# Hashed attention with an FFN beside it: GpSimd's subtractions, the hash products and a normalising multiply put at other places of a step

## The chip, the core and the metric

The program runs on one NeuronCore of a Trainium2 chip. TensorE multiplies matrices, VectorE (DVE), ScalarE (ACT) and GpSimd (POOL) work on whole tiles, and SyncE (SP) issues most transfers. Each engine takes its instructions strictly in the order in which they stand. The metric is the device time of one launch in microseconds. A profile is one such execution, recorded.

## The reference

```python
q_bits = (einsum('bhsd,dk->bhsk', q, proj) > 0)        # 6 sign bits per row: its bucket; the same for k
mask   = q_bucket[:, :, :, None] == k_bucket[:, :, None, :]
scores = where(mask, q @ k.T / 8, -1e9)
attn   = exp(scores - scores.max(-1)); attn /= attn.sum(-1) + 1e-9
x      = (attn @ v) as [3072 tokens, 512]               # 4 batches, 8 heads, 768 rows, 64 wide
h      = x @ w_in                                       # 512 -> 2048
out    = (h * clip(h + 3, 0, 6) / 6) @ w_out            # 2048 -> 512
```

All of it is in float32.

## The kernel before, in words

**Products.** TensorE multiplies float32 numbers as a high and a low part. The high part is a rounding copy (`hi`, made by ACT), the low part is what the copy lost (`lo = x - hi`, a subtraction by DVE or POOL). A product is then three matmuls, or two where one side carries both parts side by side.

**Attention.** There are 32 heads of 768 rows; a *step* `k` handles 128 query rows of one head, so a head has six steps and the program 192. What a step does is spread over its neighbours: at step `k` the scores of step `k + 3` are multiplied (`lead`, L937), the row minima of `k + 2` are taken (`lowest`, L360), the exponential of `k + 1` is formed (`exponential`, L371) and its result is turned in blocks of 32 by DVE and written to DRAM (`flip`, L395; tiles `f` and `fd`). `move` (L403) brings the turned probabilities of step `k` back in four transfers, in place as tile `spare` or `px`. Two steps later `split_p` (L420) splits them into `ph` and `pl`, in two halves: half 0 by ACT and DVE, half 1 by ACT and POOL (L442, L443). `values` (L457) then multiplies them with `v` into `acc`; it runs in even steps only, for two steps at once: twelve matmuls, alternately with `ph` (L465) and `pl` (L466).

**A new head.** When `k + 3` reaches the first step of a head, `split_qk` (L273) prepares the head after it: ACT copies (L295), three transfers repeat the high parts in other places (L296 to L298), and POOL subtracts the low parts of `k` (tile `kk`, L301) and of `q` (tile `qq`, L303). Later steps of the head load the raw tile of the next one (`get_qk`), split `v` (`split_v`, L336, L337, on POOL), multiply the hash (`hash_qk`, L305, six matmuls into the PSUM tile `z`), turn its signs into mask columns (`bits`, L314, DVE) and scale the next raw tile (`scale_q`, L267, ACT). The scores tile `s` and the hash tile `z` share one pair of PSUM banks here, so whichever comes next on TensorE waits until DVE has read the one before (`lowest` reads `s`, `bits` reads `z`).

**The FFN beside it.** From step 107 on, `beside_ffn` (L1005) writes one step of attention and one 128-column block of the FFN into each other by hand. A generator `ffn` (L827) is advanced at four stages: at A it splits the gated values (`gb`: ACT L601, POOL L602), at B it multiplies `h` (`gemm1`, L573 to L575), at C it multiplies the block before (`gemm2`, L611 to L613) and applies the gate (ACT L593, DVE L594), and at D it does one item of preparing the next 256 tokens (`beside`): broadcasting reciprocals (POOL L521), two transposes into `rt` (TensorE L531) and a multiply by `rt` (DVE L534). TensorE's row of a step is therefore: values (even steps), `h`, hash (one step in six), `po`, scores, `rt` (while tokens are prepared).

The order on TensorE, DVE, ACT and POOL is the order of this code; nothing is moved by a scheduler. SP takes the transfers in its own order. The flag `paced` is true inside `beside_ffn`, and `lows` collects the low-part subtractions of a step, which `split_lows` issues after `lead`.

Of the kernel before, what the change touches and what calls it, by code (L numbers as in the profile page):

```python
# [10 lines left out]
F32 = mybir.dt.float32  # L11
# [7 lines left out]
P = 128  # L19
# [9 lines left out]
LA = 3  # L29
# [14 lines left out]
def lsh_attention_moe(  # L44
# [10 lines left out]
    nc = tc.nc  # L55
# [3 lines left out]
    KT = S // P  # L59
# [197 lines left out]
    def spans(i: int):  # L257


        n = 4 if i <= 2 else 1  # L260
        return [slice(x * S // n, (x + 1) * S // n) for x in range(n)]
# [8 lines left out]

    copied = None

    def split_qk(i: int, copy):  # L273
# [25 lines left out]
        copied = last  # L299
        for c in spans(i + 1):  # L300
            nc.gpsimd.tensor_sub(k2[:D, c], raw[D:, c], q1[D:, c].bitcast(F32))  # L301
        for c in spans(i + 1):
            nc.gpsimd.tensor_sub(q2[D:, c], raw[:D, c], q1[:D, c].bitcast(F32))  # L303

# [115 lines left out]
    def split_p(g: int, c: int, third: bool):  # L420
# [23 lines left out]
        nc.scalar.copy(hi, pt)  # L444
        lows.append(lambda: engine.tensor_sub(lo, pt, hi.bitcast(F32)))  # L445

# [80 lines left out]
    def normalise(name: str, x, rb, tag: str | None = None):  # L527

        rt = bank([P, TC], f"rt{name}", tag)
        for u in range(TC // P):  # L530
            nc.tensor.transpose(  # L531
                rt[:, u * P : (u + 1) * P], rb[:, u].rearrange("p h d -> p (h d)"), ident[:]
            )
        nc.vector.tensor_mul(x, x, rt[:])  # L534

# [26 lines left out]

    def split_x(x, src, engine):
        nc.scalar.copy(x[0], src)  # L564
        engine.tensor_sub(x[1], src, x[0].bitcast(F32))  # L565
# [371 lines left out]
    def lead(j: int):  # L937
# [8 lines left out]
        if t == 2:  # L946
            if i:
                split_v(i)

            if n + 1 < NJ and n != H + 1:  # L950
                get_qk(n + 1)
# [5 lines left out]
        if t == 3 and n < NJ and alone:  # L957
            bits(n)
        if t == 4 and n + 1 < NJ:
            scale_q(n + 1)  # L960
# [28 lines left out]
    with tc.manual_schedule(engines={ET.PE, ET.DVE, ET.Activation, ET.Pool}):  # L989
# [9 lines left out]
        def go(part: str):  # L999
            if stage == part:  # L1000
                next(fill, None)
# [3 lines left out]
        def beside_ffn(k: int):  # L1005
# [24 lines left out]
            if k + 2 < NS:  # L1030
                lowest(k + 2)
            paced = True
            while through and (through[0] < vnext // 2 - 1 or k % 2 or k < GT):
                output(through.pop(0))
            if k + LA < NS and (k + LA) % KT == 2 and (k + LA) // KT + 1 < NJ:
                hash_qk((k + LA) // KT + 1)
                bits((k + LA) // KT + 1)
# [4 lines left out]
            if GT <= k < NS:  # L1042
                move(k)
            go("D")
            if k % KT in (2, 4):
# [124 lines left out]
```

## Time and profile before

| | us |
|---|---|
| median of 3 runs | 1073.55 |
| lowest and highest | 1073.17, 1077.03 |
| the profiled execution | 1075.23 |
| its span in the trace | 1073.5 |
| TensorE busy, mean granted clock | 992.4, 0.958 |
| VectorE, ScalarE, GpSimd busy | 690.5, 634.8, 530.8 |

The profiled execution spent 1.7 us outside its span. The page lists an instruction group with its busy time and, behind the bar, the idle time of its engine just before it with the instruction that ended it. `gb<-g,gb` reads "writes gb, reads g and gb". The clock column gives the TensorE clock that was granted, 1.00 being full speed. Roughly, the span has four parts: attention alone to 150 us, the FFN of the first batch to about 275 us, attention alone to about 420 us, attention beside the FFN (steps 107 and on) to about 885 us, and the rest of the FFN.

### The profile page before, as it was taken

The page shows a single profiled execution, that of the slowest core. Times are in us where ns is not written, and L with a number is a line of the kernel's source. Part 1 is how long each engine was busy: PE and PEld are TensorE (multiplying, and loading weights), DVE is VectorE, ACT ScalarE, POOL GpSimd, SP SyncE. Part 2 cuts the span into 40 slices and gives each one's busy share as a digit, 9 for nine tenths or more (in the row PEclk, how much of TensorE's full clock was granted, in tenths as well). Part 3 has the DMA queues.
Part 4 walks back from the last instruction along what each step waited for, and adds up shares of the span by engine and source line. Part 5 has one row for each costly group of instructions (what it writes and reads, how often), then busy time and mean ns, then how long its engine had stood idle before and what let it go on. Part 6 is the DMA issues. An engine that isn't in the chain of part 4 may idle for free.

```text
span 1073.5 us, 19263 instructions
## 1 busy us (share of the span) xinstructions
PE 992.4 (92%) x6342; PEld 901.1 (84%) x6342; DVE 690.5 (64%) x1350; ACT 634.8 (59%) x1418; POOL 530.8 (49%) x608
## 2 busy tenths in 40 slices
PE   8999999999999997788988898878988999999998
PEld 7998888888899986677877777877977888898997
DVE  7999988987599997556555565565654661233322
ACT  6888865555688885455555565555655663334332
POOL 6777726566277764555555545555555552200000
PEclk9999999999999998689998899889998999999999
DMA  4566586000355545666586667667666751001000
GB/s 125 147 148 161 142 308 221 1 1 6 104 114 118 121 119 158 197 184 203 161 226 194 198 182 208 186 201 227 188 175 195 216 163 48 22 18 41 1 21 20
DMA packets 107898, 146.78 MB, mean 137 GB/s; under 512 B 12644, under 2 KB 77540, under 8 KB 107800
## 3 DMA queue, kind: packets, MB, share of 16 engines
q1 hardware_dynamic: 103320, 140.06, 43.0%
q0 software_dynamic: 4480, 5.51, 4.5%
q8 instruction: 50, 0.82, 0.3%
q14 instruction: 48, 0.39, 0.1%
HBM read 74.98 MB, written 51.12 MB: 117 GB/s over the span
## 4 chain that ended last, share of the span: by engine, by line
PE 39%; DMA 5%; POOL 4%; issue 3%; DVE 3%; ACT 2%; SPq 2%; DVEq 0%; POOLq 0%; ACTq 0%
PE h L574 5%; PE h L575 5%; PE h L573 5%; PE po L611 5%; PE po L613 5%; PE po L612 5%; PE acc L466 3%; DMA fd<-f 2%; PE acc L465 2%; POOL qq L303 2%; SPq L78 2%; PE s L356 1%; PE s L358 1%; DVE f L398 1%; POOL pl L445 1%
## 5 line engine op out<-in xcount | busy, mean ns | idle before, releaser
L594 DVE SCALAR_TENSOR_TENSOR g<-g,h 128x256 f32<-128x256 f32 x192 | 80.5, 419 | 205.7 <-ACT g L593 205.1
L365 DVE TENSOR_SCALAR_CACHE_REDUCE p<-s 128x768 f32<-128x768 f32 x192 | 183.4, 956 | 26.3 <-PE pt L387 12.4
L593 ACT ACTIVATE g<-h,three 128x256 f32<-128x256 f32 x192 | 91.2, 475 | 177.3 <-PE h L575 154.5
L377 ACT ACTIVATE p<-p,m 128x768 f32<-128x768 f32 x192 | 179.6, 935 | 27.0 <-DVE p L365 26.3
L466 PE MATMUL acc<-pl,vv 128*128 128x256 f32 x564 | 149.7, 296 | 40.9 <-POOL pl L445 36.7
L465 PE MATMUL acc<-ph,vv 128*128 128x256 f32 x564 | 154.6, 303 | 3.3 <-DVE pl L445 3.3
L573 PE MATMUL h<-xh,w 128*128 128x256 f32 x512 | 151.2, 295 | 0.7 <-ACT xh L564 0.7
L466 PEld LDWEIGHTS acc<-pl,vv 128*128 128x128 f32 x564 | 111.2, 197 | 46.3 <-POOL pl L445 39.3
L575 PE MATMUL h<-xh,w 128*128 128x256 f32 x512 | 149.6, 292 | 0.0
L574 PE MATMUL h<-xl,w 128*128 128x256 f32 x512 | 149.4, 292 | 0.0
L602 POOL TENSOR_TENSOR gb<-g,gb 128x256 fp32r<-128x256 f32 x89 | 67.0, 752 | 127.6 <-ACT gb L601 127.6
L398 DVE STREAM_TRANSPOSE f<-p 128x768 f32<-128x768 f32 x84 | 82.0, 976 | 54.2 <-DMA fd<-f 39.6
L465 PEld LDWEIGHTS acc<-ph,vv 128*128 128x128 f32 x564 | 110.1, 195 | 6.6 <-issue 2.1
L356 PE MATMUL s<-kk,qq 76*128 76x384 f32 x384 | 103.0, 349 | 11.4 <-DVE p L365 8.0
L444 ACT CAST ph<-pt 128x384 fp32r<-128x384 f32 x208 | 93.1, 474 | 25.2 <-PE pt L387 14.3
L445 DVE TENSOR_TENSOR pl<-pt,ph 128x384 fp32r<-128x384 f32 x208 | 106.0, 549 | 2.5 <-ACT ph L444 1.9
L573 PEld LDWEIGHTS h<-xh,w 128*128 128x128 f32 x512 | 102.9, 201 | 2.7 <-ACT xh L564 1.0
L574 PEld LDWEIGHTS h<-xl,w 128*128 128x128 f32 x512 | 102.9, 201 | 1.7 <-DVE xl L565 0.2
L575 PEld LDWEIGHTS h<-xh,w 128*128 128x128 f32 x512 | 102.8, 201 | 0.0
L358 PE MATMUL s<-kk,qq 128*128 128x384 f32 x384 | 101.1, 345 | 0.0
L611 PE MATMUL po<-w,gb 128*128 128x512 f32 x242 | 100.0, 413 | 0.9 <-ACT gb L601 0.8
L613 PE MATMUL po<-w,gb 128*128 128x512 f32 x242 | 98.7, 408 | 1.2 <-POOL gb L602 0.9
(164 smaller groups left out, 2408.3 us busy)
## 6 DMA issues: line engine op xcount, KB each, us to landing
fd<-f SPq DMA_DIRECT2D x84, 384.0 KB, 2.9
spare<-fd SPq DMA_DIRECT2D x168, 96.0 KB, 2.3
px<-fd SPq DMA_DIRECT2D x168, 96.0 KB, 2.7
raw<-in_qkT SPq DMA_DIRECT2D x32, 384.0 KB, 4.3
kk<-qq SPq DMA_DIRECT2D x62, 192.0 KB, 3.1
wr<-in_w_in SPq DMA_DIRECT2D x16, 512.0 KB, 4.7
wr<-in_w_out SPq DMA_DIRECT2D x16, 512.0 KB, 11.1
vr<-in_v SPq DMA_DIRECT2D x32, 192.0 KB, 2.5
```

Of the source, the lines that this page charges most:

```text
L356: nc.tensor.matmul(s[:, c, :HW], lhsT=q1[:KM, us], rhs=half(k1[:KM], c), start=True, stop=False)
L358: nc.tensor.matmul(s[:, c, :HW], lhsT=q2[:, us], rhs=half(k2, c), start=False, stop=True)
L365: nc.vector.tensor_scalar(out=pr_[:], in0=s[:, :, :HW], scalar1=CAP, scalar2=None, op0=ALU.min, op1=ALU.min, accum_out=m[:],)
L377: nc.scalar.activation(pr_[:], pr_[:], AF.Exp, bias=m[:], scale=-1.0, accum_out=sms[b][:, t, h : h + 1])
L445: lows.append(lambda: engine.tensor_sub(lo, pt, hi.bitcast(F32)))
L465: nc.tensor.matmul(acc[:], lhsT=vv[:, kt], rhs=hi[:, x], start=(kt == 0), stop=False)
L466: nc.tensor.matmul(acc[:], lhsT=vv[:, kt], rhs=lo[:, x], start=False, stop=(kt == KT - 1))
L573: nc.tensor.matmul(hp[:], lhsT=wi[:, 0, wc], rhs=xh, start=(cc == 0), stop=False)
L574: nc.tensor.matmul(hp[:], lhsT=wi[:, 0, wc], rhs=xl, start=False, stop=False)
L575: nc.tensor.matmul(hp[:], lhsT=wi[:, 1, wc], rhs=xh, start=False, stop=(cc == NCC - 1))
L611: nc.tensor.matmul(po[u], lhsT=gh[:, us], rhs=wo[:, 0], start=(fc == 0), stop=False)
L613: nc.tensor.matmul(po[u], lhsT=gl[:, us], rhs=wo[:, 0], start=False, stop=(fc == NFC - 1))
```

## The change

All of it concerns steps in which `paced` is true, and there it does five things.

1. Where POOL makes a low part of the probabilities (half 1), the subtraction is issued directly behind ACT's copy in `split_p`. The one of DVE still waits for `split_lows`.
2. The two subtractions of `split_qk` go into a list `subs`. One is taken from it near the end of each step, after `split_lows` and `move` and before stage D, so the second runs one step later than the first.
3. `hash_qk` and `bits` run when `(k + 3) % 6` is 3, one step later than before. That step is even.
4. The load of the raw tile goes from the head's step 2 to its step 3, the scaling of it from step 4 to step 5.
5. The multiply by `rt` goes into a list `muls`; it is issued in the next step, behind `lowest`, or ahead of a split that needs it.

Three places of the order show it. On POOL, around a head's subtractions in the middle of the stage, this stood there (`gb` is the FFN's low part, `kk` and `qq` the head's, `pl` the probabilities', `spare<-rc` the broadcast):

```order
L602 TENSOR_TENSOR gb_0_10_6549<-g_0_10_6532,gb_0_10_6549 128x256
L301 TENSOR_TENSOR kk_6586<-raw_6351,qq_6587 64x768
L303 TENSOR_TENSOR qq_6587<-raw_6351,qq_6587 64x768
L445 TENSOR_TENSOR pl_1_6504<-px,ph_1_6503 128x3x128
L521 COPY spare<-rc_1_6480 128x256
L602 TENSOR_TENSOR gb_0_11_6624<-g_0_11_6583,gb_0_11_6624 128x256
L445 TENSOR_TENSOR pl_1_6631<-spare,ph_1_6630 128x3x128
```

and now this stands there:

```order
L621 TENSOR_TENSOR gb_0_10_6549<-g_0_10_6532,gb_0_10_6549 128x256
L452 TENSOR_TENSOR pl_1_6503<-px,ph_1_6502 128x3x128
L304 TENSOR_TENSOR kk_6587<-raw_6415,qq_6588 64x768
L530 COPY spare<-rc_1_6479 128x256
L621 TENSOR_TENSOR gb_0_11_6622<-g_0_11_6584,gb_0_11_6622 128x256
L452 TENSOR_TENSOR pl_1_6629<-spare,ph_1_6628 128x3x128
L304 TENSOR_TENSOR qq_6588<-raw_6415,qq_6588 64x768
```

The `pl` subtraction stands ahead of the head's, and the second of the head's stands behind the `pl` of the next step.

On DVE, some steps later, while tokens are prepared (`f` is the turn, `p` the minima, `qq<-z` the bits, `g` the gate, `pl` half 0, `xr` the multiply by `rt`), before:

```order
L534 TENSOR_TENSOR xr_1_6466<-xr_1_6466,rt_1_1_6673 128x256
L398 STREAM_TRANSPOSE f_6698<-p_6651 128x768
L365 TENSOR_SCALAR p_6703,m_6702<-s_6662 128x768
L321 TENSOR_SCALAR qq_6587<-z_6707,thr,val 44x768
L594 SCALAR_TENSOR_TENSOR g_0_13_6722<-g_0_13_6722,h_0_13_6685 128x256
L445 TENSOR_TENSOR pl_0_6628<-px,ph_0_6627 128x3x128
L534 TENSOR_TENSOR xr_1_6466<-xr_1_6466,rt_1_2_6741 128x256
L398 STREAM_TRANSPOSE f_6782<-p_6703 128x768
```

and now:

```order
L404 STREAM_TRANSPOSE f_6698<-p_6650 128x768
L371 TENSOR_SCALAR p_6703,m_6702<-s_6662 128x768
L543 TENSOR_TENSOR xr_1_6467<-xr_1_6467,rt_1_1_6673 128x256
L613 SCALAR_TENSOR_TENSOR g_0_13_6714<-g_0_13_6714,h_0_13_6685 128x256
L454 TENSOR_TENSOR pl_0_6626<-px,ph_0_6625 128x3x128
L404 STREAM_TRANSPOSE f_6771<-p_6703 128x768
L371 TENSOR_SCALAR p_6776,m_6775<-s_6720 128x768
L543 TENSOR_TENSOR xr_1_6467<-xr_1_6467,rt_1_2_6730 128x256
L327 TENSOR_SCALAR qq_6588<-z_6779,thr,val 44x768
```

The bits moved to the step behind, and each multiply by `rt` from the end of its step to the place behind the next step's minima.

The diff, whole but for lines of context:

```diff
@@ split_qk
         copied = last
-        for c in spans(i + 1):
-            nc.gpsimd.tensor_sub(k2[:D, c], raw[D:, c], q1[D:, c].bitcast(F32))
-        for c in spans(i + 1):
-            nc.gpsimd.tensor_sub(q2[D:, c], raw[:D, c], q1[:D, c].bitcast(F32))
+        for to, r in ((k2[:D], slice(D, P)), (q2[D:], slice(0, D))):
+            def low(to=to, r=r):
+                for c in spans(i + 1):
+                    nc.gpsimd.tensor_sub(to[:, c], raw[r, c], q1[r, c].bitcast(F32))
+            if paced:
+                subs.append(low)
+            else:
+                low()
@@ split_p
         nc.scalar.copy(hi, pt)
-        lows.append(lambda: engine.tensor_sub(lo, pt, hi.bitcast(F32)))
+        if engine is nc.gpsimd:
+            engine.tensor_sub(lo, pt, hi.bitcast(F32))
+        else:
+            lows.append(lambda: engine.tensor_sub(lo, pt, hi.bitcast(F32)))
@@ normalise
-        nc.vector.tensor_mul(x, x, rt[:])
+        muls.append(lambda: nc.vector.tensor_mul(x, x, rt[:]))
+        if not paced:
+            multiply()
+
+    muls = []
+
+    def multiply():
+        for f in muls:
+            f()
+        muls.clear()
@@ split_x
     def split_x(x, src, engine):
+        multiply()
@@ lead
         if t == 2:
             if i:
                 split_v(i)
+        if t == (3 if paced else 2):
             if n + 1 < NJ and n != H + 1:
                 get_qk(n + 1)
...
-        if t == 4 and n + 1 < NJ:
+        if t == (5 if paced else 4) and n + 1 < NJ:
             scale_q(n + 1)
@@ beside_ffn
             paced = True
+            multiply()
             while through and (through[0] < vnext // 2 - 1 or k % 2 or k < GT):
                 output(through.pop(0))
-            if k + LA < NS and (k + LA) % KT == 2 and (k + LA) // KT + 1 < NJ:
+            if k + LA < NS and (k + LA) % KT == 3 and (k + LA) // KT + 1 < NJ:
                 hash_qk((k + LA) // KT + 1)
                 bits((k + LA) // KT + 1)
...
             split_lows()
             if GT <= k < NS:
                 move(k)
+            if subs:
+                subs.pop(0)()
             go("D")
```

More of the change, by code (lines that the diff above doesn't have):

```diff
@@ L271, in lsh_attention_moe @@
     copied = None
+    subs = []
     def split_qk(i: int, copy):
```

## The prediction, made before the change was timed

> **What bounds the kernel now.** I read the page's first two parts first.
>
> ```profile
> PE 992.4 (92%) x6342; PEld 901.1 (84%) x6342; DVE 690.5 (64%) x1350; ACT 634.8 (59%) x1418; POOL 530.8 (49%) x608
> PEclk9999999999999998689998899889998999999999
> ```
>
> TensorE is busy for 92% of the span, and its clock reads below 9 only in slices 16 to 31 of 40, which is attention beside the FFN, the stage of the change. So I looked at that stage alone: what TensorE waited for between 470 and 820 us, most first (us, times, longest).
>
> ```profile
> PE acc L466 <- POOL pl L445: 35.6, 11, 3.6
> PE z L310 <- DVE p L365: 5.3, 4, 2.1
> PE s L356 <- DVE p L365: 2.4, 5, 0.7
> PE acc L466 <- DVE pl L445: 1.2, 2, 0.9
> ```
>
> One wait outweighs the rest: 35.6 us in eleven pieces of at most 3.6, in which the product with the probabilities' low part waits for POOL. The page's row of that product (idle time behind the bar) has 36.7 us of it in all, so nearly none lies outside this window.
>
> ```profile
> L466 PE MATMUL acc<-pl,vv 128*128 128x256 f32 x564 | 149.7, 296 | 40.9 <-POOL pl L445 36.7
> ```
>
> The timelines of POOL and TensorE show one of the eleven (start, duration, and in brackets the idle time before).
>
> ```profile
> 504.25 1.84 POOL L301 TENSOR_TENSOR kk<-raw,qq 64x768 fp32r<-64x768 f32 x1 [2.28 <-PE po L613]
> 506.14 1.80 POOL L303 TENSOR_TENSOR qq<-raw,qq 64x768 fp32r<-64x768 f32 x1
> 508.03 0.99 POOL L445 TENSOR_TENSOR pl<-px,ph 128x384 fp32r<-128x384 f32 x1
> 501.26 0.28 PE L573 MATMUL h<-xh,w 128*128 128x256 f32 x1
> 502.66 0.39 PE L611 MATMUL po<-w,gb 128*128 128x512 f32 x1
> 504.04 0.52 PE L356 MATMUL s<-kk,qq 76*128 76x384 f32 x2
> 509.07 0.58 PE L466 MATMUL acc<-pl,vv 128*128 128x256 f32 x1 [3.10 <-POOL pl L445]
> 510.31 0.41 PE L573 MATMUL h<-xh,w 128*128 128x256 f32 x1
> 512.87 0.63 PE L611 MATMUL po<-w,gb 128*128 128x512 f32 x1
> 515.32 0.52 PE L356 MATMUL s<-kk,qq 76*128 76x384 f32 x2
> ```
>
> POOL subtracts `kk` and `qq` of the next head for 3.6 us, and only then makes `pl`, which ends at 509.02; TensorE starts again at 509.07, 3.10 us late. The rows behind the wait are slower too. The twelve `h` matmuls took 1.40 us from 501.26 to 502.66 and 2.56 from 510.31 to 512.87; the six `po` matmuls 1.38 and 2.45. That is half clock, which the windows of 6.5 us behind each of the eleven waits confirm (us; busy PE, PEld, DVE, ACT, POOL; granted clock; DMA share). The first, the third and the last are shown.
>
> ```profile
> 475.60:482.10 6.50, 6.50 (x27) 6.05 (x28) 1.87 (x3) 2.27 (x6) 2.41 (x3) 0.58 0.48 127
> 545.00:551.50 6.50, 6.46 (x34) 6.09 (x34) 1.91 (x4) 2.31 (x5) 3.18 (x5) 0.74 1.06 261
> 816.20:822.70 6.50, 6.48 (x25) 5.96 (x26) 1.85 (x3) 1.91 (x5) 2.44 (x3) 0.53 0.67 186
> ```
>
> Seven of the eleven read 0.53 to 0.59, four 0.74. TensorE is busy in all of each window, so the lost clock is lost time.
>
> Last, how fast the stage runs without this. From the first resumption after such a wait to the eleventh there are ten heads; behind them, no head being left to split, comes a stretch of eight steps, from one turn of DVE (L398) to the eighth after it.
>
> ```profile
> 475.60:816.20 340.60, 297.99 (x1772) 269.91 (x1772) 195.39 (x345) 192.08 (x434) 181.77 (x203) 0.92 0.68 196
> 834.80:869.10 34.30, 33.21 (x220) 30.55 (x219) 23.73 (x45) 22.52 (x54) 17.23 (x22) 1.00 0.65 199
> 834.76 0.98 DVE L398 STREAM_TRANSPOSE f<-p 128x768 f32<-128x768 f32 x1 [2.36 <-DMA fd<-f]
> 869.08 0.97 DVE L398 STREAM_TRANSPOSE f<-p 128x768 f32<-128x768 f32 x1
> ```
>
> The ten heads took 34.06 us each, 5.68 a step; the eight steps 4.29 each, TensorE busy for 33.21 of 34.30 us at clock 1.00. So the other engines and the transfers can keep TensorE full at 4.29 us a step when a head's preparation is absent. With one hash, six matmuls of 0.17 us (a row below), that is 6 x 4.29 + 1.03 = 26.8 us for a head, 7.3 less than now.
>
> **The change part by part.** *The `pl` subtraction ahead of the head's two (edits 1 and 2).* Nothing is added: the durations of POOL's groups in the stage stay.
>
> ```profile
> L445 POOL TENSOR_TENSOR pl<-px,ph 128x384 fp32r<-128x384 f32 x31 | 31.3, 1011 | 4.6 <-ACT ph L444 1.7 <-DMA fd<-f 1.5
> L301 POOL TENSOR_TENSOR kk<-raw,qq 64x768 fp32r<-64x768 f32 x11 | 21.0, 1911 | 22.5 <-PE po L613 13.9 <-issue 4.8 <-ACT qq L295 3.8
> L303 POOL TENSOR_TENSOR qq<-raw,qq 64x768 fp32r<-64x768 f32 x11 | 20.1, 1832 | 0.6
> L602 POOL TENSOR_TENSOR gb<-g,gb 128x256 fp32r<-128x256 f32 x61 | 45.8, 751 | 79.0 <-ACT gb L601 79.0
> ```
>
> In front of the `pl` that TensorE waits for, 1.91 + 1.83 = 3.74 us go away; the waits were 3.24 on average (35.6 / 11), so all of it goes: **-35.6**. Is `pl` then early enough? It needs ACT's copy of half 1. TensorE was done with the product before it at 505.97 at the latest (3.10 us ahead of 509.07), and POOL had stood idle for 2.28 us before 504.25: there is room for 1.01 us.
>
> The clock loss behind the waits goes with them. Seven windows lose about 0.44, four 0.26: (7 x 0.44 + 4 x 0.26) x 6.5 = 26.8 us of full-speed work. At half clock the rows above took 1.8 times, not twice, so a little less was lost in time: 26.8 x 0.44 / 0.5 = 23.6; I take **-24**. Bounds: none, if what remains of the waits still cools the clock, and 26.8.
>
> In sentences that the sum does without: the Trainium skill, page TensorE: Matmul & The Clock Gate, section HAM oscillation, has the array fall to half clock after idle gaps above about 3.4 us, its window running freely. By that a wait of 3.24, the average here, would cost no clock, and the term would be near nothing instead of 24, the time 1045. The rows disagree: half clock stands behind a wait of 3.10 us here, and behind all eleven. The trace's term stays.
>
> The two subtractions now stand elsewhere, 1.9 us each, at the ends of two steps. Behind the first stands `gb` (L602) of the next step, which TensorE asks for in the `po` group, behind twelve `h` and twelve value matmuls of the same shape, 2.8 us into the step. Behind the second stands the `gb` of a step without values, asked for 1.4 us into it. POOL waits 1.3 us a step for `gb`'s copy (79.0 / 61), so a subtraction delays `gb` by about 0.6, and the matmuls ahead hide that: nothing. If that cover is gone it is at most 1.9 us a head, 21 us. The hash needs `qq` only in the step after the next.
>
> *The hash in an even step (edit 3).* The hash waits until DVE has taken the minima from the shared banks.
>
> ```profile
> 518.91 0.40 PE L310 MATMUL z<-qq,pjl 128*108 128x384 f32 x1 [1.09 <-DVE p L365]
> 519.84 0.34 PE L312 MATMUL z<-qq,pjh 128*108 128x384 f32 x1
> DVE qq L321 <- PE z L312: 14.1, 10, 1.5
> ```
>
> In an odd step only the `h` matmuls (1.4 us) stand between the scores and the hash; in an even one 1.4 us of values come in addition. The four waits here were 1.1 to 2.1 us, so about 1.4 us of cover takes nearly all: **-5**. In exchange DVE waits longer for `z`, which already costs it 1.4 us a time (14.1 / 10), and its gate and low part come later in that step. Scores follow the hash by 1.4 us of `po`, the bits take 1.09 us: it fits. Bounds: -5.3 and, if DVE is late into the next, shorter step by all of the 1.4, +15.
>
> *The raw tile a step later (edit 4)*: loaded for two steps (9 us) ahead of its scaling.
>
> ```profile
> raw<-in_qkT SPq DMA_DIRECT2D x9, 384.0 KB, 4.3
> fd<-f SPq DMA_DIRECT2D x68, 384.0 KB, 3.0
> ```
>
> It lands 4.3 us after issue: nothing. *The multiply by `rt` (edit 5)* takes a wait off DVE.
>
> ```profile
> DVE xr L534 <- PE rt L531: 13.9, 16, 1.9
> DVE f L398 <- DMA fd<-f: 25.0, 19, 2.2
> ```
>
> 13.9 us in 16 pieces, off TensorE's path while TensorE is full: nothing, but DVE reaches its turn 0.9 us earlier in those steps. The PSUM bank of `rt` is held for about one step more. There are four banks in turn and two or three tiles a step, so it comes round after that.
>
> **What is late next.** The turn (`f`) may overwrite its tile only when the write before it has landed; DVE waited 25.0 us for that in 19 turns. The chain of a step is: turn 0.98, issue of the write, landing 3.0, that is 4.3 us with SP free; TensorE needs 26.8 / 6 = 4.47. They are nearly equal. A head's three copies and its raw load stand in SP's queue in just those steps whose stall vanishes, and there a write takes longer. I put the new waits at 1.0 us a head: **+11**. Bounds: 0, and 3.75 a head (rival A), +41; I stay nearer to the lower, because the eight full steps hold such writes too. Denser traffic is in it: a DMA share of 0.68 over 34.06 us becomes 0.68 x 34.06 / 29 = 0.80.
>
> **Sum**: 35.6 + 24 + 5 - 11 = 53.6. The profiled execution took 1075.23 us, 1073.5 in its span; 1075.2 - 53.6 = 1021.6. The median was 1.7 us below that execution, and the gain should show in the median as well, so I say **1021 us** (1073.55 - 53.6 = 1020; between the two). The first head of the stage, before 470 us, is left out; it lost about 1 us to the same wait. The FFN after 885 us has nothing of the change.
>
> **The rivals.**
>
> *A. The write of the turn paces half of the steps.* SP issues four transfers for `move` ahead of the next write.
>
> ```profile
> 577.99 1.74 SPq L78 DMA_DIRECT2D px<-fd  x4
> 441.30 0.45 SPq L78 DMA_DIRECT2D fd<-f  x1
> 446.32 0.98 DVE L398 STREAM_TRANSPOSE f<-p 128x768 f32<-128x768 f32 x1 [2.83 <-DMA fd<-f]
> 448.44 0.65 PE L310 MATMUL z<-qq,pjl 128*108 128x384 f32 x1 [3.57 <-DVE p L365]
> ```
>
> They take 1.74 us of SP. Where DVE's turn follows its low part at once, the chain is 0.98 + 1.74 + 3.0 = 5.72 us, 1.25 over TensorE's 4.47. In three steps of a head this makes 3.75 us, 41 over the stage: 1021 + 41 - 11 = **1051**. For it: 19 waits on that write already. Against it: the eight full steps above contain such writes as well. The Trainium skill, DMA: Bandwidth & Descriptors, section Queues, rings and completion order, says that each DMA engine takes one issuer's descriptors in ring order; by that the head's copies are served ahead of the write behind them. The rows agree: the write issued at 441.30 landed at 446.3, after 5.0 us instead of 3.0.
>
> *B. The stall returns at another place.* The last three rows are one: a late write, DVE idle for 2.83 us, TensorE for 3.57, and half clock behind it. That costs 3.57 + 24 / 11 = 5.8 us; one for each of eleven heads is 64 us, and the time stays at **1074**. It needs a landing some 2 us later than usual, which the three copies (192 KB each) and the raw load could bring; against it, none of the 19 waits between 470 and 820 us was longer than 2.2.
>
> *C. Slower.* The same mechanism twice a head, in the step of the copies and in that of the raw load: 22 x 5.8 = 127 instead of the 64 removed, **1137**. It decides where two writes of a head land over 5 us after their issue. At one a head it is B.
>
> *D. `pl` isn't the last thing that half 1 waits for.* If ACT's copy, behind its own waits, is late by 2 us, TensorE waits 2 instead of 3.24 and keeps its clock: 22 us stay, 1021 + 22 = **1043**. Against it: POOL's `pl<-px` waited for ACT 1.7 us in 31 times.
>
> **How the numbers follow.** My forecast 0.68 (own range 1007 to 1034: -11 for no new waits, -3 for the clock's upper bound; +13 for new waits of 2.2 a head), A 0.14 and D 0.08 (1034 to 1058), B 0.05, C 0.03, and 0.02 for a gain under 15 us from mixtures. The range 1005 to 1050 leaves out half of A, B, C and the mixtures above, 0.17, and about 0.03 below. A median can be told from no change at 0.5%, 5.4 us, so faster means below 1068: 0.68 + 0.22 + 0.02 = 0.92. Same 0.05, slower 0.03.
>
> **What would show it.** TensorE's wait on POOL's `pl` in the stage falls from eleven pieces to none or some below 1 us; the clock column reads 9 throughout the stage but for its first two slices; POOL shows `pl` directly behind ACT's copy and `gb` between the head's two subtractions; the hash waits for the minima for under 2 us in all; the stage runs at 4.7 to 4.9 us a step; the FFN behind it has its old length. I am wrong if TensorE's waits for `p` (L365 of before) grow past 25 us, which is A or B; if the clock stays below 0.9 though the waits went; or if `po` waits for `gb` in the step of a subtraction, which breaks the cover that I named.

## The result

The changed kernel took **1047.47 us** (median of four, 1045.37 to 1049.28) beside 1073.36 for the kernel before on the same chip, a ratio of 0.975, interval 0.972 to 0.979. It is faster, inside the range, and 26 us above the time of the likeliest case. About half of the forecast gain came. 1047 is next to the time of rival A, 1051.

The first two parts of the page of the changed kernel, in the rows that answer to those of before, and its chain by line:

```profile
PE 979.4 (94%) x6342; PEld 885.6 (85%) x6342; DVE 706.9 (68%) x1350; ACT 634.6 (61%) x1418; POOL 534.1 (51%) x608
PEclk9999999999999999699999999999998999999999
...
DMA fd<-f 6%; PE h L593 6%; PE h L594 5%; PE h L592 5%; PE pt L393 5%; PE acc L474 5%; PE acc L475 5%; PE po L630 5%; PE po L632 5%; PE po L631 5%; PE s L362 4%; PE s L364 4%; DMA px<-fd 3%; DVE p L371 3%; SPq L78 3%
```

The clock reads 9 in the stage but for slices 17 and 31, where before it was below 9 in eight. The chain that ended last names the write of the turn, `fd<-f`, first. To put both kernels on one footing I took ten heads of each, from hash to hash (length, busy PE, PEld, DVE, ACT, POOL, granted clock, DMA share, GB/s). Before:

```profile
448.40:790.00 341.60, 299.35 (x1768) 271.63 (x1768) 193.54 (x341) 189.99 (x428) 177.78 (x197) 0.91 0.67 195
```

After:

```profile
449.40:768.20 318.80, 286.33 (x1770) 255.86 (x1770) 207.12 (x342) 190.30 (x429) 183.20 (x200) 0.97 0.72 209
```

What TensorE waited for in the ten heads, before:

```profile
PE acc L466 <- POOL pl L445: 32.0, 10, 3.6
PE z L310 <- DVE p L365: 7.8, 4, 3.6
PE s L356 <- DVE p L365: 2.4, 5, 0.7
PE acc L466 <- DVE pl L445: 1.2, 2, 0.9
```

And after, all rows of the view:

```profile
PE z L316 <- DVE p L371: 14.1, 8, 4.4
PE s L362 <- DVE p L371: 11.0, 9, 3.6
PE acc L475 <- DVE pl L454: 2.4, 3, 1.4
PE po L632 <- POOL gb L621: 1.7, 4, 0.4
PE po L630 <- ACT gb L620: 1.5, 3, 1.0
```

POOL's `pl` is gone without a rest. In its place the hash (`z`) and the scores (`s`) wait 14.1 + 11.0 = 25.1 us for the minima (`p`, L371, once L365), which were 7.8 + 2.4 = 10.2.

A head takes 31.88 us instead of 34.16. Of the 22.8 us in ten heads, TensorE's busy time gave 13.0 (299.35 to 286.33, for the same work) and its idle time 9.8 (42.25 to 32.47). The idle time should have fallen by the 32.0 of the stall, and the waits for the minima took back 25.1 - 10.2 = 14.9 of it; the sum at the end of this document has the rest.

The clock rose from 0.91 to 0.97 and not to 1. Two of the new waits, by the timeline:

```profile
542.54 0.84 PE L362 MATMUL s<-kk,qq 76*128 76x384 f32 x2 [3.62 <-DVE p L371]
706.29 0.42 PE L316 MATMUL z<-qq,pjl 128*108 128x384 f32 x1 [4.42 <-DVE p L371]
```

And the 6.5 us behind each, and behind one of 1.62 us at 572.56 (its row stands below), of which the third number from the end is the clock:

```profile
542.60:549.10 6.50, 6.50 (x36) 6.45 (x37) 2.82 (x6) 3.41 (x7) 2.06 (x3) 0.74 0.59 191
572.60:579.10 6.50, 6.50 (x34) 6.18 (x35) 3.13 (x7) 3.30 (x7) 2.51 (x4) 0.74 0.74 256
706.30:712.80 6.50, 6.50 (x30) 5.88 (x31) 3.83 (x6) 2.54 (x7) 1.66 (x2) 0.74 0.32 99
```

Behind most of the shorter ones the clock is full. So the new waits are more than the old, but smaller, and only some of them still cool the array. Who is late is read from DVE's own waits in the ten heads:

```profile
DVE f L404 <- DMA fd<-f: 55.7, 31, 5.3
```

The same stretch of before had:

```profile
DVE f L398 <- DMA fd<-f: 26.4, 20, 2.3
```

The turn now waits 55.7 us for the write before it, twice the 26.4 of before, and once for 5.3. That is not all. The same views put a further 11.6 us of the turn's waits (2.1 before) down to ACT's `ph` and `gb`. In each of them the trace has the last part of the write landing 0.09 us ahead of the turn, as in the rows that name the write, so they are waits for the write too: 67.3 us against 28.5. Where the trace tells when a transfer landed (10 of the 71 writes from 480 to 860 us, and 5 of 68 before), the median is not longer (3.0 us before, as quoted in the prediction):

```profile
fd<-f SPq DMA_DIRECT2D x71, 384.0 KB, 2.7
```

What is longer is the way to the issue and the worst landings, as one head shows. The timeline of the changed kernel there, by engine (start, duration, idle time before in brackets):

```profile
564.74 0.98 DVE L404 STREAM_TRANSPOSE f<-p 128x768 f32<-128x768 f32 x1 [2.02 <-DMA fd<-f]
567.06 1.49 DVE L454 TENSOR_TENSOR pl<-spare,ph 128x384 fp32r<-128x384 f32 x1
570.43 0.98 DVE L404 STREAM_TRANSPOSE f<-p 128x768 f32<-128x768 f32 x1 [1.88 <-ACT ph L450]
575.84 0.98 DVE L404 STREAM_TRANSPOSE f<-p 128x768 f32<-128x768 f32 x1 [2.02 <-DMA fd<-f]
...
565.20 1.02 POOL L452 TENSOR_TENSOR pl<-spare,ph 128x384 fp32r<-128x384 f32 x1
566.29 1.84 POOL L304 TENSOR_TENSOR qq<-raw,qq 64x768 fp32r<-64x768 f32 x1
...
564.48 2.04 SPq L78 DMA_DIRECT2D px<-fd  x4
566.62 0.67 SPq L78 DMA_DIRECT2D fd<-f  x1
568.61 1.75 SPq L78 DMA_DIRECT2D spare<-fd  x4
570.46 0.38 SPq L78 DMA_DIRECT2D raw<-in_qkT  x1
571.44 0.34 SPq L78 DMA_DIRECT2D fd<-f  x1
...
572.56 0.62 PE L362 MATMUL s<-kk,qq 76*128 76x384 f32 x2 [1.62 <-DVE p L371]
```

Two things can be read here. First, the turn at 564.74 ends at 565.72, but SP is still issuing the four `move`s of `px`, and the write goes out at 566.62. Second, DVE's own `pl` (half 0) starts at 567.06 while POOL is in the head's second subtraction (`qq`, 566.29 to 568.13), and takes 1.49 us; the mean before was 0.55. It ends at 568.55, and SP's next `move` overwrites the tile that it reads, so it goes out at 568.61. Behind that stand the raw load (570.46) and the next write (571.44); the turn that needs this write's landing comes at 575.84, 4.40 us later. This write was issued 0.03 us behind the end of its turn (570.43 + 0.98), so what stands ahead of it can have made it land late, but not leave late. (The wait of 1.88 us that the row at 570.43 puts down to ACT is one of those for the write, issued at 566.62.) In all ten subtractions from `spare` that were held for over 1 us in the stage, the `move` came 0.06 to 0.07 us behind the end of the subtraction.

The collision is a consequence of the change that the prediction did not have. Before, both head subtractions ended ahead of POOL's `pl`, and DVE's `pl` of that kind took 551 ns on average over the 30 of the ten heads. So after the result there were two readings of the missing 26 us. One, called W below: rival A, the chain of turn, issue, landing and next turn paces the steps of the copies whatever else is done. Two, called P: the collision does it, and without it the forecast would have come. A third, called H, was the hash: in its even step it might be what pulled the minima apart.

### The profile page after: what moved, and what is told of

The parts are those of the page before. It is cut to its first block, busy times and chain, and to the rows that moved or that the text cites. A ratio compares the mean times of both kernels' runs of the same rounds, so it can differ in the third digit from the quotient of the medians.

```text
span 1045.8 us, 19273 instructions
## 1 busy us (share of the span) xinstructions
PE 979.4 (94%) x6342; PEld 885.6 (85%) x6342; DVE 706.9 (68%) x1350; ACT 634.6 (61%) x1418; POOL 534.1 (51%) x608
## 4 chain that ended last, share of the span: by engine, by line
PE 58%; DVE 13%; DMA 12%; ACT 6%; issue 5%; SPq 3%; POOL 3%; DVEq 0%; ACTq 0%; POOLq 0%
DMA fd<-f 6%; PE h L593 6%; PE h L594 5%; PE h L592 5%; PE pt L393 5%; PE acc L474 5%; PE acc L475 5%; PE po L630 5%; PE po L632 5%; PE po L631 5%; PE s L362 4%; PE s L364 4%; DMA px<-fd 3%; DVE p L371 3%; SPq L78 3%
## 5 line engine op out<-in xcount | busy, mean ns | idle before, releaser
L371 DVE TENSOR_SCALAR_CACHE_REDUCE p<-s 128x768 f32<-128x768 f32 x192 | 183.4, 955 | 26.9 <-PE pt L393 12.4
L475 PE MATMUL acc<-pl,vv 128*128 128x256 f32 x564 | 147.2, 292 | 6.3 <-DVE pl L454 6.1
L592 PE MATMUL h<-xh,w 128*128 128x256 f32 x512 | 146.8, 287 | 0.7 <-ACT xh L583 0.7
L593 PE MATMUL h<-xl,w 128*128 128x256 f32 x512 | 145.3, 284 | 0.9 <-POOL xl L584 0.7
L594 PE MATMUL h<-xh,w 128*128 128x256 f32 x512 | 144.9, 283 | 0.0
L593 PEld LDWEIGHTS h<-xl,w 128*128 128x128 f32 x512 | 98.3, 192 | 3.4 <-POOL xl L584 1.2
L592 PEld LDWEIGHTS h<-xh,w 128*128 128x128 f32 x512 | 98.5, 192 | 2.7 <-ACT xh L583 1.0
L632 PE MATMUL po<-w,gb 128*128 128x512 f32 x242 | 97.4, 403 | 3.0 <-POOL gb L621 2.4
L630 PE MATMUL po<-w,gb 128*128 128x512 f32 x242 | 96.6, 399 | 2.5 <-ACT gb L620 2.5
L594 PEld LDWEIGHTS h<-xh,w 128*128 128x128 f32 x512 | 98.1, 192 | 0.0
```

The costliest lines, as they stand in the source:

```text
L371: nc.vector.tensor_scalar(out=pr_[:], in0=s[:, :, :HW], scalar1=CAP, scalar2=None, op0=ALU.min, op1=ALU.min, accum_out=m[:],)
L475: nc.tensor.matmul(acc[:], lhsT=vv[:, kt], rhs=lo[:, x], start=False, stop=(kt == KT - 1))
L592: nc.tensor.matmul(hp[:], lhsT=wi[:, 0, wc], rhs=xh, start=(cc == 0), stop=False)
L593: nc.tensor.matmul(hp[:], lhsT=wi[:, 0, wc], rhs=xl, start=False, stop=False)
L594: nc.tensor.matmul(hp[:], lhsT=wi[:, 1, wc], rhs=xh, start=False, stop=(cc == NCC - 1))
L630: nc.tensor.matmul(po[u], lhsT=gh[:, us], rhs=wo[:, 0], start=(fc == 0), stop=False)
```

## The experiments

Unless a text says otherwise a ratio is against the kernel before, timed in the same group of runs, with its 95% interval; since its median moved between groups (1073.36, 1071.19, 1074.83), kernels of different groups are compared by ratio. A ratio of 0.01 is 10.7 us. The changed kernel stands at 0.975 [0.972, 0.979]. The expectations are on record as they were written, under the names that they give to the three readings above.

**Edit 1 alone**, in the kernel before:

```diff
-        lows.append(lambda: engine.tensor_sub(lo, pt, hi.bitcast(F32)))
+        if engine is nc.gpsimd:
+            engine.tensor_sub(lo, pt, hi.bitcast(F32))
+        else:
+            lows.append(lambda: engine.tensor_sub(lo, pt, hi.bitcast(F32)))
```

> The kernel before with edit 1 alone: POOL's low part of half 1 directly behind ACT's copy; the head's two subtractions, the hash, the raw tile and the multiply stay where they were. Theory W (once POOL's low part is early, the stage is paced by the write of the turn, which must land before the next turn): nearly the whole gain comes from this edit, 1046 to 1051 us, and DVE waits some 50 us or more for the write. Theory P (in the changed kernel the head's second subtraction holds up DVE's own subtraction, 1.8 us instead of 0.55, and so the transfers behind it): there is no such collision here, so it is faster than the changed kernel, 1038 to 1043. Theory H (the hash in the even step costs waits of its own): faster than the changed kernel too, TensorE's waits of the hash for the minima 5 to 8 us instead of 15.

1042.61 us, 0.973 [0.970, 0.977]. What TensorE waited for longest in its ten heads (445.3 to 757.5 us):

```profile
PE z L310 <- DVE p L365: 20.0, 11, 4.8
```

And DVE for the write:

```profile
DVE f L398 <- DMA fd<-f: 23.8, 19, 2.4
```

This one edit brings the whole gain; the four others together add nothing that can be told from zero. Here the subtractions don't collide (`pl<-spare` 552 ns). The turn's row for the write is no longer than before (23.8), but with the 14.1 us put down to ACT's `ph` and `gb`, which are waits for the write here too, it is 37.9 us against 28.5. So the waits for the write grow without the collision too, though less than in the changed kernel (67.3). The time is the one that P gave, yet it can't be told from the changed kernel's. H had 5 to 8 us of waits of the hash for its odd step; there are 20.0.

**The hash back in the odd step**, in the changed kernel:

```diff
-            if k + LA < NS and (k + LA) % KT == 3 and (k + LA) // KT + 1 < NJ:
+            if k + LA < NS and (k + LA) % KT == 2 and (k + LA) // KT + 1 < NJ:
```

> The changed kernel with edit 3 alone undone: hash and bits in the odd step again, the rest as changed. H: the waits of the hash for the minima fall from 15.3 us to 5 or 6 and the time by 6 to 10, to 1037 to 1041 us. W: the late minima then hold up the scores instead, the sum of the waits for the minima stays at 27 to 32 us and the time at 1045 to 1050. My prediction had this edit at -5, so by it 1052.

1047.42 us, 0.978 [0.974, 0.982]: no difference. TensorE's waits for the minima only change places, in its ten heads:

```profile
PE z L316 <- DVE p L371: 23.6, 9, 4.4
PE s L362 <- DVE p L371: 1.8, 4, 1.0
```

25.4 us instead of 25.1, nearly all now at the hash. So the hash's place is not what costs, and in this kernel it is not worth the 5 us forecast either.

**The head's subtractions in four pieces each:**

```diff
-                for c in spans(i + 1):
+                for c in spans(0 if paced else i + 1):
```

> The changed kernel, but each of the head's two subtractions in four pieces of 192 columns, so that DVE is held up by a piece and not by a whole subtraction. P: DVE's subtraction in that step takes 0.6 to 1.0 us instead of 1.5 to 1.8 and the time falls by 6 to 12 us, to 1036 to 1041. W: DVE's subtraction gets shorter, but the time stays within 3 us of 1047.

1039.08 us, 0.970 [0.965, 0.976]. In its ten heads DVE's `pl<-spare` took 626 ns on average, 916 in the changed kernel, so the hold is shorter. But the pieces of a head take POOL 5.07 us instead of 3.80, and a new wait for `gb` stands at `po`:

```profile
PE po L632 <- POOL gb L621: 10.7, 10, 1.5
```

The time is in P's range, but the interval overlaps with the changed kernel's, so alone this settles nothing.

**Both subtractions in one step**, at its end, so that the second meets no `pl` of DVE from `spare`:

```diff
-            if subs:
+            while subs:
                 subs.pop(0)()
```

> The changed kernel, but both of the head's subtractions at the end of the same step, the split in two steps undone. P: POOL then begins them behind DVE's subtraction of that step, the collision is gone and the time falls by 5 to 10 us, to 1038 to 1042. W: 1045 to 1050. If the split in two steps was needed, TensorE waits for POOL's gb or pl in the step behind, by up to 1.9 us a head, and the time is 1050 to 1065.

1032.48 us, 0.963 [0.960, 0.966]: 13 us faster than the changed kernel, with intervals apart, and more than P gave.

Its ten heads, and in the next view DVE's subtraction from `spare`:

```profile
449.30:754.70 305.40, 282.93 (x1773) 251.39 (x1771) 200.86 (x342) 190.04 (x428) 183.62 (x201) 0.99 0.75 218
```

```profile
L454 DVE TENSOR_TENSOR pl<-spare,ph 128x384 fp32r<-128x384 f32 x30 | 16.5, 551 | 0.1
```

The hold at `spare` is gone (part of it is now at `px`, 773 ns for 651), the clock is 0.99, and DVE still waits 35.9 us for the write, 55.9 with the rows that name ACT's `ph` and `gb`. Moving the second subtraction is worth about 13 us of the 26 missing, not all.

One more thing moves with it. The raw load overwrites the tile that the head's subtractions read, so it can't go before the second of them has ended. In the changed kernel SP issues it behind the four `move`s, 0.5 to 2.4 us ahead of the next write in each of the ten heads, and from the issue of that write to the turn that needs it there are 4.36 us on average. In this run the load goes ahead of the `move`s, 3.6 to 5.9 us before the write, and there are 3.43 us. SP in the same head as above:

```profile
561.80 0.38 SPq L78 DMA_DIRECT2D fd<-f  x1
562.27 0.38 SPq L78 DMA_DIRECT2D raw<-in_qkT  x1
564.21 1.75 SPq L78 DMA_DIRECT2D spare<-fd  x4
566.43 0.34 SPq L78 DMA_DIRECT2D fd<-f  x1
```

In the two further runs on the collision (the fill, and the second subtraction ahead of `pl`) the load goes early too, with 3.49 and 3.62 us. So these runs show what the place of the second subtraction costs. How much of it is the hold on DVE and how much the place of the raw load, none of them shows; in the run with four pieces, where the hold is short, the load still stood right ahead of the write in seven of ten heads.

**A fill with zeros instead of the second subtraction**, in its place of the changed kernel. The low part of `q` is left out of the scores and the hash:

```diff
             def low(to=to, r=r):
+                if paced and r.start == 0:
+                    nc.gpsimd.memset(to.bitcast(F32), 0.0)
+                    return
```

> The changed kernel, but in the stage beside the FFN the second of a head's subtractions (the low part of q) is replaced at its place by a fill with zeros, which reads nothing. It leaves the low part of q out of the scores and the hash of those heads. P (POOL's second subtraction holds DVE's own up): DVE's subtraction into pl takes 0.55 to 0.65 us on average instead of 0.93, the waits for the minima fall from 29.7 to below 18 us, and the time to 1028 to 1038 us, at or below the version with both subtractions in one step (1032.5). W (the write of the turn paces the stage whatever POOL does): DVE's subtraction gets shorter, the waits for the minima stay at 25 us or more, 1043 to 1048.

1036.06 us, 0.967 [0.963, 0.971].

The groups of POOL and, in the next view, of DVE:

```profile
L304 POOL MEMSET qq<- 64x768 f32 x10 | 7.4, 736 | 0.6
```

```profile
L457 DVE TENSOR_TENSOR pl<-spare,ph 128x384 fp32r<-128x384 f32 x30 | 16.5, 551 | 0.0
```

An instruction of POOL that reads nothing does not hold DVE: 551 ns. The two overlapped by only 0.03 to 0.45 us a head, though, where the second subtraction overlapped by 0.39 to 1.79. The run gains about 9 us, inside P's range, and the waits for the minima from 455 to 800 us are 18.0 us for 29.7. That is no more than moving the subtraction gave, though the whole 1.84 us of POOL's reading is gone too.

**One step, and the hash in the odd step** (both edits above):

> Both subtractions in one step (1032.5 us) and the hash back in the odd step. With the collision away the hash edit should show what it is worth. My prediction: the four to eleven waits of the hash come back at 1 to 2 us each, 1037 to 1045 us. If the waits for the minima only move between hash and scores, as they did in the changed kernel (1047.4 against 1047.5), 1031 to 1035.

1043.9 us, 0.975 [0.972, 0.979], as expected. With this run four kernels differ only in two edits:

| ratio to before | hash in the even step | hash in the odd step |
|---|---|---|
| subtractions in two steps | 0.975 (the change) | 0.978 |
| subtractions in one step | 0.963 | 0.975 |

TensorE's longest wait by its sum in the ten heads of the new kernel:

```profile
PE z L316 <- DVE p L371: 16.8, 11, 3.7
```

From the upper right corner neither edit alone gains more than 0.3%, and the two together 1.5%. With the hash odd TensorE waits 16.8 us at the hash anyway; with the subtractions in two steps it waits for late minima wherever the hash is. The hash's even place is worth 13 us once the second subtraction is moved, and nothing that shows before; and moving it is worth 13 us only with the hash in the even step.

**One step, and the multiply by `rt` where it was before** (edit 5 undone):

```diff
         muls.append(lambda: nc.vector.tensor_mul(x, x, rt[:]))
-        if not paced:
-            multiply()
+        multiply()
```

> Both subtractions in one step (1032.5 us) and the multiply by rt back at the end of its step. My prediction: DVE waits some 12 to 14 us for the transposes again, off TensorE's path, so 1031 to 1035 us. If the turn's start now decides (W), 16 multiplies that end 0.4 to 0.9 us later put the writes and the minima late, 1037 to 1046.

1035.89 us, 0.967 [0.964, 0.971] beside 0.963 [0.960, 0.966]: the intervals overlap, so edit 5 is worth 0 to some 5 us; the time lies between the two ranges. DVE's wait for `rt` is back with 9.6 us.

**The turn in place.** The tiles `f` and `p` have two buffers between them and are made alternately, so every turn writes the buffer that the write just before it reads. If DVE turns `p` where it lies, no tile `f` is needed, each `p` has a buffer to itself for two steps, and what has to wait for that write is the minima, which come one turn later (1.1 us). With both subtractions in one step:

```diff
-        x = sp.tile([P, S], F32, name=f"f{g}", tag="p", bufs=2)
-        nc.vector.transpose(x[:], probs.pop(g)[0][:].rearrange("p c k -> p (c k)"))
+        x = probs.pop(g)[0][:].rearrange("p c k -> p (c k)")
+        nc.vector.transpose(x, x)
         d = dp.tile([P, S], F32, name=f"fd{g}", tag="fd", bufs=4)
-        dma(out=d[:], in_=x[:])
+        dma(out=d[:], in_=x)
```

> Both subtractions in one step (1032.5 us), and the turn writes in place of what it reads, so that not the turn but the minima behind it, 1.0 us later, must wait for the write before. W: of DVE's 40 us of waits for the write in 29 pieces about 1 us each goes, TensorE's waits for the minima (9.5 us) halve, 1022 to 1029 us. If the transfers themselves are the bound (how much they move, not when), DVE's wait goes from the turn to the minima in full and the time stays at 1030 to 1035.

1021.44 us, 0.954 [0.951, 0.958], below the kernel without it by 9 us with intervals apart, and just below the range that W gave. The raw load goes ahead of the `move`s in both of these kernels, so this pair has the slack of the write alone.

**The second subtraction ahead of POOL's `pl`** of its step, everything else as in the change, so that it runs ahead of DVE's subtraction:

```diff
             go("A")
+            if subs:
+                subs.pop(0)()
...
-            if subs:
+            if len(subs) == 2:
                 subs.pop(0)()
```

> The changed kernel with one instruction of POOL at another place: the head's second subtraction stands in the same step as now, but ahead of POOL's low part of half 1 and not behind it, so it runs some 1.0 us and more before DVE's subtraction comes up. P: DVE's subtraction into pl takes 0.55 to 0.65 us on average in the tile where it now takes 0.93, and the time falls to 1028 to 1036 us. W: 1044 to 1049. If POOL's low part, now 1.9 us later in that step, is what the transfers behind it wait for, also 1044 or more.

1038.83 us, 0.967 [0.964, 0.970]: 9 us faster by the place of one instruction on POOL, but less than P expected. A part of the hold stays:

```profile
L454 DVE TENSOR_TENSOR pl<-spare,ph 128x384 fp32r<-128x384 f32 x30 | 19.1, 636 | 0.1
```

**The change with the turn in place**, the collision untouched:

> The changed kernel with the turn in place (the wait for the write goes from the turn to the minima behind it, 1.0 us later); the collision of POOL's second subtraction stays. If collision and write act one behind the other in the same step (the held subtraction makes the transfers late, the late transfers the turn), the gain is at least that of the one-step version (11 us): 1030 to 1037. If the collision alone decides, 1043 to 1048.

**1019.46 us**, 0.948 [0.945, 0.952].

Its ten heads, then DVE's subtraction, then DVE's wait for the write (now at the minima), then TensorE's waits for the minima:

```profile
446.50:739.20 292.70, 277.43 (x1771) 250.47 (x1772) 201.29 (x342) 188.46 (x427) 183.92 (x201) 0.99 0.79 226
```

```profile
L454 DVE TENSOR_TENSOR pl<-spare,ph 128x384 fp32r<-128x384 f32 x30 | 26.3, 876 | 0.3
```

```profile
DVE p L371 <- DMA fd<-p: 26.4, 22, 4.0
```

```profile
PE z L316 <- DVE p L371: 6.2, 4, 2.7
PE s L362 <- DVE p L371: 4.4, 4, 2.6
```

This run weighs most against P. DVE's subtraction is held nearly as before (876 ns on average for 916), and still 29 us go, 26.1 of them in the ten heads; both ranges had allowed less. TensorE's waits for the minima fall from 25.1 to 10.6 us, and DVE's for the write from 67.3 to 26.4. The 29 us are not the slack alone: SP's order differs too, and the raw load goes out behind that write in nine of the ten heads, not right ahead of it. Two pairs have the load at one place: the one-step kernels, above, gain 9 us from turning in place, and the kernel before, below, 16. In all three pairs the slack shortens the time, so the chain through the write was what paced. The hold on DVE costs nothing that shows once this chain has about 1 us of slack (0.948 with the hold; 0.954 and, below, 0.951 in the two kernels in place that lessen it).

**The kernel before with the turn in place:**

> The kernel before with the turn in place and nothing else. POOL's low part then still comes 3.2 us late once a head, and the half clock follows; the write was hidden by that stall. So 1066 to 1074, no change within 0.7%. If the write had paced the steps already before the change, 1055 to 1064.

1058.63 us, 0.985 [0.981, 0.989]. I had expected no change, and it gains 1.5%, which lies in the range for the case that the write had paced already before the change.

Its ten heads, and TensorE's longest wait in them:

```profile
447.00:776.80 329.80, 290.86 (x1769) 266.09 (x1769) 189.63 (x341) 189.30 (x428) 177.13 (x197) 0.94 0.69 201
```

```profile
PE acc L466 <- POOL pl L445: 31.5, 10, 3.5
```

The stall at `pl` stays as it was, 31.5 us in ten. Of the 11.8 us gained in ten heads, 8.5 are TensorE's busy time at the better clock (0.94 for 0.91) and 3.3 idle time. Half clock behind a stall was shorter: over the 6.5 us behind each of the ten stalls the granted clock read 0.53 to 0.59 six times before, and here 0.55 to 0.57 three times and 1.00 once, the rest 0.74 to 0.76. Why it was shorter is not settled, and each figure is from one execution.

**Turn in place and the second subtraction ahead of `pl`:**

> The turn in place, and the head's subtractions in two steps with the second ahead of POOL's low part (e9 and e10 together). Against the one-step version in place (1021.4 us) gb should be late only once a head by 0.6 us or less: TensorE's waits of po for gb fall from 7.1 us to 2 or less, and the time to 1013 to 1020 us. If two subtractions in two steps cost DVE more than the one run of both, 1022 to 1028.

1019.44 us, 0.951 [0.946, 0.955]. DVE's `pl<-spare` is 604 ns, the waits for POOL's `gb` are 2.1 us for 7.1 in the one-step kernel in place, as expected, and the time is that of the run with the collision. It is the same statement from the other side.

The steps of a head show where all this lies. Here is the mean distance from one turn to the next over ten heads, by place in the head. The stall at `pl` fell into the fourth column, the hash follows the turn that begins the last one (in the kernel before it stands one step earlier):

| us | 1 | 2 | 3 | 4 | 5 | 6 | head |
|---|---|---|---|---|---|---|---|
| before | 4.09 | 4.36 | 5.23 | 8.84 | 5.92 | 5.69 | 34.1 |
| the change | 5.23 | 4.21 | 4.68 | 6.06 | 5.82 | 5.88 | 31.9 |
| both subtractions in one step | 5.13 | 4.25 | 4.87 | 6.06 | 4.54 | 5.70 | 30.6 |
| the change, turn in place | 3.42 | 5.63 | 3.84 | 5.18 | 4.54 | 6.65 | 29.3 |

The change leaves three steps at 5.8 to 6.1 us and has the other three at 4.2 to 5.2, which is the shape that rival A gave (5.72 in three steps, the rest at TensorE's pace). Moving the second subtraction away shortens the fifth by 1.3. In place, the turns come in uneven pairs and the sum is what matters.

## Why the prediction came out so

The time lies in the forecast's range, but above the part that the likeliest case had of it, 1007 to 1034, in the part kept for A and D. By the signs that it had named the forecast did not come: the waits for the minima passed 25 us, the hash waited 14.1 us instead of under 2, and a step took 5.31 us (31.88 / 6) instead of 4.7 to 4.9. That the range holds the time is owed to its width, not to the mechanism.

**Right: the wait itself.** All 35.6 us at POOL's `pl` went, the subtraction stands early enough (rival D did not come: no row with `pl` from POOL is left), and the first edit alone shows it.

**Right in kind, too small in size: "new waits +11".** This is the step that failed. It said that the chain of turn, issue and landing was nearly equal to TensorE's pace and took 1.0 us a head for what would come late. The waits for the minima grew by 14.9 in ten heads (to 29.7 from 455 to 800 us, past the 25 that I had named as the mark of A or B), and the turn's waits for the write by 38.8 (28.5 to 67.3). The landing of 3.0 us in the chain was the median of the five writes whose landing the trace tells. The argument for staying near the lower bound was the eight steps at 4.29 us behind the last head. They do contain writes, but no copies, no raw load and no head subtraction, so they couldn't speak for the three steps that have them. That argument was also the one used against rival A, and A's sum of 1051 is 4 us from the time. Its chance of 0.14 was too low; the two quantities it compared, 5.72 and 4.47, stood in the prediction, while 19 waits already there were counted as a minor point. That A's sum comes so near is luck in part: one of the three slow steps, the fifth, is slow here through the second subtraction's new place (5.82 us, 4.54 with both in one step), which A does not have.

**Mis-sized for the same reason: the clock, -24.** Over ten heads TensorE's busy time fell by 13.0, where the term gives 24 x 10 / 11 = 21.8. The bound "if what remains of the waits still cools the clock" is what happened in part: waits of 2.3 to 4.4 us were all followed by a lower clock (the three of the ten heads, 0.74 to 0.75 over 6.5 us), and of seven waits between 1.1 and 1.8 us two were. I had the Trainium skill's rule (TensorE: Matmul & The Clock Gate, section HAM oscillation: gaps above about 3.4 us) set aside for the trace; the rows of after keep to that, since 2.30 us is below it and was followed by 0.75. By the rule only the waits of 3.62 and 4.42 within the ten heads would have cooled. The size of the term was right for a stage without such waits: in the changed kernel with the turn in place TensorE's busy time in ten heads is 277.43, which is 21.9 below that of before.

**Wrong: the two subtractions cost "nothing".** The cover that I named was for `gb`, and it held: TensorE's waits for POOL's `gb` are 1.7 us in all. What I didn't look at was DVE, which makes the other half of `pl` in the same moment. The second subtraction holds it once a head, and the three kernels in which that hold is gone or short are 9 to 13 us faster (0.963 in one step, 0.967 with the fill, 0.967 ahead of `pl`). In the same three the raw load leaves earlier, so the hold's own part of this is not shown. The order of either engine tells nothing of the hold; the two timelines side by side would have.

**Mis-sized: the hash, -5.** It is 0 in the changed kernel and about 13 with both subtractions in one step. The term assumed that the minima come when they did before. Its bound on the other side, DVE late into the next step, shows in the first column, 4.09 us before and 5.23 after: with the hash alone put back in its odd step that column is 4.41.

**The multiply by `rt`, 0**: between 0 and 5 us, not settled. **The raw tile, 0**: not tried apart. In all ten heads its load stands right ahead of a write, which then takes 4.36 us to the turn that needs it; with both subtractions in one step, and the edit kept, the load is out of the way (3.43). So it takes the late second subtraction to put it there.

B and C did not come, though single waits of B's size did (3.62 and 4.42 in ten heads).

**The FFN at the end** kept its length, as forecast: 199.2 us from the last turn to the end of the span before, 200.5 after.

The sum by what was measured, for ten heads: 32.0 for the stall and 13.0 for TensorE's busy time, less 14.9 for the minima, 3.5 for DVE's `pl` and for `gb` (5.6 now, 2.1 before) and 3.8 of gaps that no wait is listed for, is 22.8. The span fell by 27.7: 1.0 was lost ahead of the ten heads, 7.1 gained between them and the last turn, and 1.2 lost behind it. Ten elevenths of the forecast's 53.6 are 48.7, so 25.9 did not come: 9.4 at the waits for the minima, the hash's part included, 8.8 at the clock, 3.5 at DVE's `pl` and at `gb`, 3.8 in those gaps and 0.4 at the stall.

## What to carry to other kernels

When a stall on one engine goes, compare the next-longest chain in the very steps that had the stall, not in quiet steps elsewhere: here a chain of 5.7 us through a DRAM write stood behind a TensorE pace of 4.5. Look for the buffer that closes that chain. Two tiles that share two buffers gave each write no slack, and turning in place brought 9 to 29 us, and in the changed kernel more (29) than the change itself (26). When a view puts a wait down to an engine that has no part in it, look for the transfer: here that hid 11.6 of 67.3 us. And see what else an edit moves: a subtraction that ends later also holds back the load that overwrites what it reads. When work is moved on POOL, look at what DVE does at that moment, and not only at what POOL does next.

## What the runs showed of the hardware

A subtraction on DVE with both inputs in SBUF is held by a subtraction that POOL has begun before it: 0.81 to 2.20 us instead of 0.55 in the ten heads of the changed kernel, ending 0.41 to 0.42 us behind POOL's end. Where DVE's had begun first it took 0.55, with up to 0.52 us of overlap. A fill on POOL, which reads nothing, held it not at all (551 ns). The Trainium skill says so (SBUF — State Buffer, section Who interferes with whom): a DVE instruction with two SBUF inputs contends with a GpSimd instruction that reads SBUF, not with one that only writes it. The rows shown agree.

Half clock stood behind waits well below those at which I had placed it: behind 1.62 us in the head shown (0.74 over the next 6.5 us), but not behind 1.79, 1.71 and 1.60 in other heads. Longer waits were no surer: behind 2.75 us in the changed kernel with the turn in place, and behind 3.32 us in the kernel before with it, the clock was 1.00. What tells them apart is open.

The turn of a 128 x 768 tile on DVE, in blocks of 32, works in place in the same 0.98 us.
